# The second copy of the convolution weights: made by VectorE inside SBUF, or by DMA transfers

## The chip, the core and the metric

The kernel runs on one core of a Trainium2 chip. The metric is device time in microseconds (us) for one execution; less is better. A core has five engines that run side by side and wait for each other by semaphores: TensorE (PE in the profile, with its weight loads as PEld), VectorE (DVE), ScalarE (ACT), GpSimd (POOL) and SyncE (SP), which here issues the DMA transfers. SBUF is the on-chip memory of 128 partitions; PE writes its results to PSUM, which here is used as eight banks.

## The reference

An image x of 1 x 224 x 224 pixels and 96 channels is convolved with a 7 x 7 kernel w of 96 x 96 channels, cyclically in both directions, by way of the Fourier transform, all in bf16 at the ends:

```python
wp = jnp.pad(w, ((0, H - K), (0, W - K), (0, 0), (0, 0)))
Xf = rfft2(x, axes=(1, 2)); Wf = rfft2(wp, axes=(0, 1))
Yf = jnp.einsum('bhwi,hwio->bhwo', Xf, Wf)
y = irfft2(Yf, s=(H, W), axes=(1, 2)).astype(jnp.bfloat16)
```

## The kernel before, in words

The kernel transforms along the rows of the image only (H, in blocks of 28 rows with 6 rows of overlap, 17 frequencies) and does the seven taps along W as a short convolution with fewer products. Per frequency there are up to three planes (real, imaginary and their combination), 50 slots in all, and per slot ten combined taps. The image goes through in seven tiles of 32 columns. In each tile 17 rounds, one for each frequency, multiply transformed pixels (J, xf) with transformed weights (WF); the sums (u, v, yf) go out to memory, come back in another order (tt), and are transformed back with a matrix G.

Every engine call goes through `call` at lines 87 to 92, which keeps the program order on each engine. So the profile gives line 88 for everything, and the groups are told apart by tiles: **wu** fillers, **wq** weights, **WF** transformed weights, **Fm** the transform matrix, **xf** transformed pixels, **J** their sums, **ct** small constants, **pb** a PSUM bank.

What the change touches is the head, before round 0:

- **Loads (178 to 197).** SyncE issues, in this order: the columns left of the image (xh), the first tile's pixels of the upper half (load_x(0, 0)), the weights, and the first tile's pixels of the lower half (load_x(0, 1)). The first tile's pixels lie in the late part of WF, which is needed only later. One queue takes them in turn.
- **The weights.** w has 49 taps of 96 x 96 channels. Tap r goes to row 2r of the tile wq: the last tap in two small transfers (185), the others in three pieces of the columns (188). The odd rows 2r + 1 hold the same weights moved by 48 output channels (C2): four transfers from wq to wq (189 to 192), each of which has to wait for its piece of w. With both copies one matmul handles two output channels at once: `prep_jobs` (349) takes a strided column o of wq as the stationary operand, for o in 0 to 47, and the matrix Em as the moving one, 98 rows contracted; Em (57 and 295) has zeros such that the even rows give the lower 48 output channels and the odd rows the upper 48. Each job makes four output pairs in one bank. The zeros behind the weights (zw, 228) let the stationary operand read 128 columns.
- **Constants.** POOL and DVE compute Fm, Em and G from iota, floors and sines. thp (245) is the tap's row, pm, twp, hf, mk, mk2 (265 to 275) the mask by tap and by parity of the row. `build_g` (299) makes G on POOL over many one-element operations, which end in a sine on ACT and a multiply on POOL (`fin`, 342), called at line 779. Small constants lie in the pool stmp, which is given back at line 780 for yf and the sums.
- **The order at the head (761 to 779).** Fillers on a zero tile, 8 and 9 (207), then the transform of the left columns (a_bank), the first tile's upper half (f_jobs, ten banks), then 20 fillers in three banks (769), then the first group of the weight transform (`prep_jobs(0)`, 12 banks of 4 matmuls), the first part of the lower half, and J of the first frequencies. The other weight groups are spread over the rounds by `add` and `pace`.
- **Who empties a bank (119).** `evac` gives a bank to DVE or ACT by two running accounts, load["v"] and load["a"], so what is booked on one engine pushes later banks to the other. The accounts are set anew at line 783, before the rounds.

Of the kernel before, what the change touches and what calls it, by code (L numbers as in the profile page):

```python
# [9 lines left out]
F32 = mybir.dt.float32  # L10
ALU = mybir.AluOpType
ACTF = mybir.ActivationFunctionType

KT = 7
B = 28
# [7 lines left out]
Q = 2 * LC  # L23
# [6 lines left out]
NTAP = 10  # L30
# [25 lines left out]
def kernel(  # L56
# [7 lines left out]
    _, H, W, C = x.shape  # L64
# [4 lines left out]
    R = HB + PAD  # L69
    PW = KT * KT  # L70
    FR = 2 * NS
    PW2 = 2 * PW
    C2 = C // 2
    assert NJ == 8
    SYNC = mybir.DependencyInfo(mybir.DependencyClass.Sync, mybir.DependencyReason.DATA)
# [57 lines left out]
    def dma(out_ap, in_ap):  # L133
        return DE.dma_start(out=out_ap, in_=in_ap)
# [40 lines left out]
    def load_x(t, jg):  # L175
        return load_rows(xbuf(t, jg), jg, t * 2 * TW, 2 * TW)

    wsrc = w.rearrange("kh kw i o -> (kh kw) (i o)")
    for jg in range(2):
# [2 lines left out]
    cuts = tuple((c * WC // 3, (c + 1) * WC // 3) for c in range(3))  # L182
    lr = PW - 1
    wp = WC // 16
    wdma = [dma(wqx[2 * lr:2 * lr + 1, 0:WC].rearrange("p (a h b) -> p a h b", a=8, h=2)[:, :, h],
                bass.AP(wsrc.tensor, wsrc.offset + lr * WC + h * wp, [[WC, 1], [2 * wp, 8], [1, wp]])) for h in range(2)]
    for c0, c1 in cuts:
        wdma.append(dma(wqx[0:2 * lr:2, c0:c1], wsrc[0:lr, c0:c1]))
    wdma.append(dma(wqx[2 * lr + 1:PW2, 0:WC - C2].rearrange("p (a b) -> p a b", a=16),
                    wqx[2 * lr:2 * lr + 1, C2:WC].rearrange("p (a b) -> p a b", a=16)))  # L190
    for c0, c1 in cuts:
        wdma.append(dma(wqx[1:2 * lr:2, max(c0 - C2, 0):c1 - C2], wqx[0:2 * lr:2, max(c0, C2):c1]))

    def beside_w(r):
        for d in wdma:
            tc.declare_no_dep(r.ins, d.ins, reason="columns behind the weights")
    load_x(0, 1)

    wu = cpool.tile([128, 128], BF16, name="wu")
# [9 lines left out]

    ntmp = [0]  # L210

    def ftile(shape):
        ntmp[0] += 1
        return stmp.tile(shape, F32, name=f"ct{ntmp[0]}")

    def iota(ap, pattern, base=0, cm=0):
        GE.iota(ap, pattern=pattern, base=base, channel_multiplier=cm, allow_small_or_imprecise_dtypes=True)
# [4 lines left out]
        VE.tensor_single_scalar(out=out_ap, in_=out_ap, scalar=MAGIC, op=ALU.subtract)  # L222

    pi_t = ftile([128, 1])
    VE.memset(pi_t[:], math.pi)
    dmy = ftile([128, 1])
    SE.activation(out=dmy[:], in_=pi_t[:], func=ACTF.Sin, bias=0.0, scale=0.0)
# [4 lines left out]
    twc = ftile([PW2, KT]); mf = ftile([R, JG, NS * 2])  # L232
    iota(nrj[:], [[-B, JG]], base=-1, cm=1)
    iota(pw_i[:], [[0, 1]], cm=1)
    iota(aa[:], [[2, NS], [0, 2]])
    iota(phf[:], [[0, NS], [LC // 2, 2]], base=LC // 2)
    iota(phe[:], [[0, NS], [-(LC // 2), 2]], base=LC // 2)
# [4 lines left out]
        eng.tensor_scalar(out=out_ap, in0=out_ap, scalar1=MAGIC, scalar2=MAGIC, op0=ALU.add, op1=ALU.subtract)  # L242

    VE.tensor_scalar(out=nrj[:], in0=nrj[:], scalar1=0.0, scalar2=float(LC - 1), op0=ALU.max, op1=ALU.min)
    floor_div(VE, thp[:], pw_i[:], 2 * KT)
    VE.memset(aa[:, 0, 1:2], float(LC))
    VE.memset(aa[:, NS - 1, :], 0.0)
    VE.memset(phf[:, 0:NS:NS - 1, 1:2], LC / 2.0)
# [4 lines left out]
    floor_div(VE, fl[:], qq[:], Q)  # L253
    VE.scalar_tensor_tensor(out=qq[:], in0=fl[:], scalar=-float(Q), in1=qq[:], op0=ALU.mult, op1=ALU.add)
    SE.activation(out=qq[:], in_=qq[:], func=ACTF.Sin, bias=pi_t[:R, :], scale=-2.0 * math.pi / Q)

    GE.memset(mf[:], 1.0)
    GE.affine_select(out=mf[:], in_=mf[:], pattern=[[-B, JG], [0, NS * 2]], compare_op=ALU.is_ge, fill=0.0, base=-1, channel_multiplier=1)
# [3 lines left out]
        o = mf[:, :, 2 * NS - 2 + r:2 * NS - 1 + r]  # L262
        GE.affine_select(out=o, in_=o, pattern=[[-B, JG], [0, 1]], compare_op=ALU.not_equal, fill=v, base=-n, channel_multiplier=1)
    iota(twc[:], [[1, KT]])
    pm = ftile([PW2, 1]); twp = ftile([PW2, 1]); hf = ftile([PW2, 1]); mk = ftile([PW2, NTAP]); mk2 = ftile([PW2, 2, NTAP])
    th14 = ftile([PW2, 1])
    GE.tensor_single_scalar(out=th14[:], in_=thp[0:PW2], scalar=-2.0 * KT, op=ALU.mult)
    GE.tensor_tensor(out=pm[:], in0=th14[:], in1=pw_i[0:PW2], op=ALU.add)
    floor_div(GE, twp[:], pm[:], 2)
    GE.tensor_single_scalar(out=th14[:], in_=twp[:], scalar=-2.0, op=ALU.mult)  # L270
    GE.tensor_tensor(out=hf[:], in0=th14[:], in1=pm[:], op=ALU.add)
    GE.tensor_scalar(out=mk[:, 0:KT], in0=twc[:], scalar1=twp[:, 0:1], scalar2=None, op0=ALU.is_equal)
    GE.tensor_tensor(out=mk[:, KT:NTAP], in0=mk[:, 0:6:2], in1=mk[:, 1:6:2], op=ALU.add)
    GE.tensor_scalar(out=mk2[:, 1], in0=mk[:], scalar1=hf[:, 0:1], scalar2=None, op0=ALU.mult)
    GE.tensor_tensor(out=mk2[:, 0], in0=mk[:], in1=mk2[:, 1], op=ALU.subtract)
    for xb in xh_bufs:
        GE.memset(xb[:, PAD * C:], 0.0)
    for xb in x0_bufs + xn_bufs:
# [12 lines left out]
    for r, k in ((0, KT - 1), (1, 0)):  # L291
        VE.tensor_single_scalar(out=pv[:, NS - 2, r:r + 1], in_=thp[0:PW2], scalar=float(k), op=ALU.is_equal)
    VE.tensor_tensor(out=pv[:, :, 2], in0=pv[:, :, 0], in1=pv[:, :, 1], op=ALU.subtract)
    ke = -(-512 // (NB * NTAP))
    for k0, k1 in ((0, ke), (ke, NSLOT)):
        beside_w(VE.tensor_tensor(out=Em[:, :, k0:k1], in0=pe3[:, k0:k1].unsqueeze(1).unsqueeze(3).to_broadcast([PW2, 2, k1 - k0, NTAP]),
# [2 lines left out]
    def build_g(nj):  # L299
        PG = nj * FR  # L300

        def floor_g(out_ap, in_ap, d):
            GE.tensor_scalar(out=out_ap, in0=in_ap, scalar1=1.0 / d, scalar2=-(d - 1) / (2.0 * d), op0=ALU.mult, op1=ALU.add)
            GE.tensor_single_scalar(out=out_ap, in_=out_ap, scalar=MAGIC, op=ALU.add)
            GE.tensor_single_scalar(out=out_ap, in_=out_ap, scalar=MAGIC, op=ALU.subtract)

        def mod_g(out_ap, in_ap, fl_ap, d):
            floor_g(fl_ap, in_ap, d)
            GE.tensor_single_scalar(out=out_ap, in_=fl_ap, scalar=-float(d), op=ALU.mult)
            GE.tensor_tensor(out=out_ap, in0=out_ap, in1=in_ap, op=ALU.add)  # L310
        p = ftile([PG, 1]); sp = ftile([PG, 1]); rm = ftile([PG, 1]); jp = ftile([PG, 1]); rr = ftile([PG, 1]); z = ftile([PG, 1])
        iota(p[:], [[0, 1]], cm=1)
        mod_g(rm[:], p[:], jp[:], FR)
        mod_g(rr[:], rm[:], sp[:], 2)
        GE.tensor_single_scalar(out=z[:], in_=sp[:], scalar=0.0, op=ALU.is_equal)
        zr = ftile([PG, 1]); ag = ftile([PG, 1]); pg = ftile([PG, 1]); amp = ftile([PG, 1]); pgt = ftile([PG, 1])
        GE.tensor_tensor(out=zr[:], in0=z[:], in1=rr[:], op=ALU.mult)
        GE.tensor_scalar(out=ag[:], in0=zr[:], scalar1=LC / 2.0, scalar2=sp[:, 0:1], op0=ALU.mult, op1=ALU.add)
        en = ftile([PG, 1]); ne = ftile([PG, 1]); tg = ftile([PG, 1])
        GE.tensor_single_scalar(out=en[:], in_=sp[:], scalar=NS - 1.0, op=ALU.is_equal)  # L320
        GE.tensor_scalar(out=ne[:], in0=en[:], scalar1=-1.0, scalar2=1.0, op0=ALU.mult, op1=ALU.add)
        GE.tensor_scalar(out=ag[:], in0=ag[:], scalar1=2.0, scalar2=ne[:, 0:1], op0=ALU.mult, op1=ALU.mult)
        GE.tensor_tensor(out=pgt[:], in0=rr[:], in1=zr[:], op=ALU.subtract)
        GE.tensor_tensor(out=pgt[:], in0=pgt[:], in1=ne[:], op=ALU.mult)
        GE.tensor_scalar(out=pg[:], in0=pgt[:], scalar1=LC / 2.0, scalar2=LC / 2.0, op0=ALU.mult, op1=ALU.add)
        GE.tensor_scalar(out=amp[:], in0=z[:], scalar1=-1.0 / LC, scalar2=2.0 / LC, op0=ALU.mult, op1=ALU.add)
        GE.tensor_tensor(out=amp[:], in0=amp[:], in1=ne[:], op=ALU.mult)
        GE.tensor_tensor(out=amp[:], in0=amp[:], in1=en[:], op=ALU.add)
        GE.tensor_scalar(out=tg[:], in0=rr[:], scalar1=B - 1.0, scalar2=PAD - 1.0, op0=ALU.mult, op1=ALU.add)
        GE.tensor_tensor(out=tg[:], in0=tg[:], in1=en[:], op=ALU.mult)  # L330
        GE.tensor_single_scalar(out=jp[:], in_=jp[:], scalar=2.0 * B, op=ALU.mult)
        GE.tensor_tensor(out=tg[:], in0=tg[:], in1=jp[:], op=ALU.add)
        nm = ftile([PG, nj, B]); jc = ftile([PG, nj, B]); msk = ftile([PG, nj, B]); fl = ftile([PG, nj, B]); th = ftile([PG, nj, B])
        iota(nm[:], [[0, nj], [1, B]], base=PAD - 1)
        iota(jc[:], [[2 * B, nj], [0, B]])
        GE.tensor_scalar(out=msk[:], in0=nm[:], scalar1=en[:, 0:1], scalar2=None, op0=ALU.mult)
        GE.tensor_tensor(out=msk[:], in0=msk[:], in1=jc[:], op=ALU.add)
        GE.tensor_scalar(out=msk[:], in0=msk[:], scalar1=tg[:, 0:1], scalar2=amp[:, 0:1], op0=ALU.is_equal, op1=ALU.mult)
        GE.tensor_scalar(out=nm[:], in0=nm[:], scalar1=ag[:, 0:1], scalar2=pg[:, 0:1], op0=ALU.mult, op1=ALU.add)
        mod_g(th[:], nm[:], fl[:], Q)  # L340

        def fin():
            SE.activation(out=th[:], in_=th[:], func=ACTF.Sin, bias=pi_t[0:PG, :], scale=-2.0 * math.pi / Q)
            GE.tensor_tensor(out=G.rearrange("p (j m) -> p j m", j=nj), in0=th[:], in1=msk[:], op=ALU.mult)
        return fin

# [415 lines left out]
    for jg in range(2):  # L762
        for f in a_bank(0, xf0, xh_bufs[jg], 0, 3, jg, 0):
            f()
    fj = [f_jobs(0, p) for p in range(3)]
    for p in range(3):
        for f in fj[p][0]:
            f()
    for n in (9, 9, 2):
        warm(n)  # L770
    for f in prep_jobs(0):
        f()
# [3 lines left out]
            tc.add_manual_dep(d.ins, last[0].ins.name, SYNC, reason="second tile's pixels later")  # L776
    for f in jit(0, 0):
        f()
    g_fin()
    stmp_cm.__exit__(None, None, None)  # L780
    yf_pool = ctx.enter_context(tc.tile_pool(name="yf", bufs=YBUF))
    tv_pool = ctx.enter_context(tc.tile_pool(name="tv", bufs=2))
# [34 lines left out]
    bursts[(NS + LAG - 3, 1)] = (2, 0)  # L817
    nburst = len(bursts)
    for r in range(NS + LAG):
        if r == 0:  # L820
            add(0, 4, fj[1][1] + fj[2][1])
        for p in range(3):
# [152 lines left out]
```

## Time and profile before

| what | us |
|---|---|
| median of 3 runs | 262.58 (261.45 to 262.92) |
| the profiled execution | 261.39 |
| its span, first to last instruction | 259.7 |
| PE busy | 250.1 (96% of the span) |
| DVE busy | 213.8 (82%) |
| ACT busy | 197.9 (76%) |
| POOL busy | 107.8 (42%) |
| granted PE clock, mean | 0.996 |

The profile is one execution, with times from the start of its span. A timeline line gives start, duration from the first to the last of a run of like instructions, engine, operation, output tile <- input tiles, shapes, count and, in brackets, the idle time before it and what ended it. A busy PE is not PE at its peak, since matmuls overlap. Where prose speaks of the trace's landings, it means the time at which the last of a transfer's 16 completion signals came.

### The profile page before, as it was taken

What the parts mean: (1) busy time and instruction counts of PE and PEld (TensorE: products, weight loads), DVE (VectorE), ACT (ScalarE), POOL (GpSimd) and SP (SyncE); (2) the same over time, 40 slices, a digit from 0 to 9 for tenths busy, and PEclk for the clock granted to TensorE, in tenths of its full rate; (3) what the DMA queues carried; (4) which work ended last, traced back from release to release, by engine and by line L of the source; (5) the groups of instructions that cost most, each with busy time, mean ns of one, the idle gap of its engine ahead of it and who ended that gap; (6) DMA issues with size and microseconds to landing.
All of it is one profiled execution on the core that took longest, in us unless ns stands there. A gap on an engine that the chain in (4) does not pass through costs nothing.

```text
span 259.7 us, 12201 instructions
## 1 busy us (share of the span) xinstructions
PE 250.1 (96%) x5156; PEld 234.3 (90%) x5156; DVE 213.8 (82%) x455; ACT 197.9 (76%) x499; POOL 107.8 (42%) x172
## 2 busy tenths in 40 slices
PE   8999998999999999999999999999999999999981
PEld 3679998999999999999999998999999999999961
DVE  5649999798978979977988788777978889889982
ACT  5548997668875667998988879989798886666662
POOL 7784123336446543334133322543133332555621
PEclk9999999999999999999999999999999999999998
DMA  6947010731111299888979549697969853595145
GB/s 166 254 126 208 24 49 3 209 113 48 48 48 61 96 254 194 247 237 254 284 213 231 161 122 301 197 264 159 321 232 208 225 172 135 142 172 165 53 117 177
DMA packets 41416, 43.44 MB, mean 167 GB/s; under 512 B 30836, under 2 KB 33104, under 8 KB 41362
## 3 DMA queue, kind: packets, MB, share of 16 engines
q1 hardware_dynamic: 41044, 41.98, 58.7%
q8 instruction: 40, 0.66, 1.1%
q0 software_dynamic: 192, 0.52, 0.7%
q10 hardware_dynamic: 126, 0.17, 0.2%
q14 instruction: 14, 0.11, 0.1%
HBM read 22.09 MB, written 19.66 MB: 161 GB/s over the span
## 4 chain that ended last, share of the span: by engine, by line
PE 82%; DVE 6%; issue 4%; ACT 3%; POOL 3%; DVEq 0%; POOLq 0%; ACTq 0%
PE pb L88 82%; POOL ct L88 2%; DVE J L88 2%; ACT WF L88 1%; DVE xf L88 1%; DVE u L88 1%; POOL yf L88 1%; DVE v L88 1%; DVE WF L88 1%; ACT xf L88 1%; DVE wq L88 1%; DVE yf L88 0%; ACT tt L88 0%; ACT tt__1860 L88 0%; ACT tt__1159 L88 0%
## 5 line engine op out<-in xcount | busy, mean ns | idle before, releaser
L88 PE MATMUL pb<-WF,J 96*128 96x96 bf16 x2782 | 160.4, 206 | 0.1
L88 PEld LDWEIGHTS <-J 96*128 96x128 bf16 x2782 | 136.5, 98 | 7.0 <-issue 0.2
L88 POOL TENSOR_TENSOR yf<-v,u 128x384 bf16<-128x384 f32 x70 | 69.8, 1011 | 124.1 <-issue 67.8
L88 ACT CAST xf<-pb 96x408 bf16<-96x408 f32 (+2 forms) x147 | 68.8, 487 | 8.7 <-PE pb L88 6.9
L88 PE MATMUL pb<-WF,xf 96*128 96x96 bf16 x991 | 61.4, 206 | 0.8 <-ACT xf L88 0.5
L88 DVE TENSOR_TENSOR J<-xf 96x1824 bf16<-96x1824 bf16 (+1 forms) x82 | 56.8, 732 | 0.1
L88 PEld LDWEIGHTS <-xf 96*128 96x128 bf16 x991 | 48.9, 98 | 1.4 <-ACT xf L88 0.6
L88 PE MATMUL pb<-Fm,xn 118*128 118x136 bf16 (+3 forms) x640 | 45.5, 199 | 0.8 <-DVE u L88 0.8
L88 ACT CAST WF<-pb 96x480 bf16<-96x480 f32 (+1 forms) x57 | 28.4, 579 | 4.7 <-PE pb L88 4.6
L88 PE MATMUL pb<-tt,Gm 102*84 102x384 bf16 (+1 forms) x132 | 32.0, 325 | 0.0
L88 PEld LDWEIGHTS <-xn 118*128 118x128 bf16 x640 | 30.5, 97 | 1.1 <-issue 1.0
L88 ACT CAST yo<-pb 84x384 bf16<-84x384 f32 (+1 forms) x65 | 27.8, 484 | 2.8 <-PE pb L88 2.8
L88 ACT CAST J<-pb 84x384 bf16<-84x384 f32 (+1 forms) x65 | 28.0, 484 | 2.5 <-PE pb L88 2.5
L88 DVE TENSOR_TENSOR J<-J 96x912 bf16<-96x912 bf16 (+2 forms) x41 | 22.8, 556 | 0.0
L88 PE MATMUL pb<-wq 98*128 98x120 bf16 (+1 forms) x288 | 21.3, 226 | 0.2 <-DMA wq<-wq 0.2
L88 PEld LDWEIGHTS <-wq 98*128 98x128 bf16 x288 | 19.4, 148 | 0.7 <-issue 0.7
L88 POOL TENSOR_TENSOR xn<-v,u 128x384 bf16<-128x384 f32 x12 | 10.9, 925 | 9.2 <-DVE J L88 6.2
L88 DVE CAST WF<-pb 96x480 bf16<-96x480 f32 (+1 forms) x15 | 8.8, 614 | 4.2 <-PE pb L88 4.0
L88 PE MATMUL pb<-wu 128*128 128x512 bf16 x39 | 10.8, 438 | 1.1 <-DVE ct L88 1.1
L88 DVE TENSOR_TENSOR yf<-v,u 128x384 bf16<-128x384 f32 x20 | 11.2, 558 | 0.7
L88 PEld LDWEIGHTS <-Gm 102*84 102x84 bf16 (+1 forms) x132 | 11.4, 118 | 0.2
L88 ACT COPY xf<-xf 96x816 bf16<-96x816 bf16 (+3 forms) x18 | 10.3, 630 | 0.0
(406 smaller groups left out, 253.5 us busy)
## 6 DMA issues: line engine op xcount, KB each, us to landing
scr<-yf SPq DMA_DIRECT2D x30, 288.0 KB
xn<-in_x_dram SPq DMA_DIRECT2D x12, 672.0 KB
tt<-scr SPq DMA_DIRECT2D x24, 336.0 KB
out_dram<-yo SPq DMA_DIRECT2D x12, 252.0 KB
out_dram<-J SPq DMA_DIRECT2D x12, 252.0 KB
tt<-scr SPq DMA_DIRECT2D x6, 288.0 KB
WF<-in_x_dram SPq DMA_DIRECT2D x2, 672.0 KB
scr<-yf SPq DMA_DIRECT2D x6, 192.0 KB
```

The lines of the kernel that those rows point to most:

```text
L88: r = fn(*a, **k)
```

## The change

The rows of wq are laid out anew: the weights themselves go to rows 64 to 112, the copy moved by 48 channels to rows 0 to 48, and rows 49 to 63 are a gap that has to be zero (cleared from row 32 on, before the copy is written). 113 rows are contracted instead of 98. The four transfers from wq to wq are gone. In their place `shift` makes three copies on DVE, one for each piece of the columns, after the fourth, seventh and tenth pixel bank; each books 600 on DVE's account. The gap is cleared by one copy on ACT and two memsets on DVE. The mask follows: POOL loses the operations on parity and gains a memset and two copies; DVE gains two operations for the tap index. 20 fillers become 4. G's last two operations move to the start of round 2, and the tiles they read (msk, th, and pi in pi_g) to pools that live longer.

```diff
-    PW2 = 2 * PW
+    UP = 64
+    PW2 = UP + PW
...
-    wdma = [dma(wqx[2 * lr:2 * lr + 1, 0:WC]...
+    wdma = [dma(wqx[UP + lr:UP + lr + 1, 0:WC]...
     for c0, c1 in cuts:
-        wdma.append(dma(wqx[0:2 * lr:2, c0:c1], wsrc[0:lr, c0:c1]))
-    wdma.append(dma(wqx[2 * lr + 1:PW2, 0:WC - C2].rearrange("p (a b) -> p a b", a=16),
-                    wqx[2 * lr:2 * lr + 1, C2:WC].rearrange("p (a b) -> p a b", a=16)))
-    for c0, c1 in cuts:
-        wdma.append(dma(wqx[1:2 * lr:2, max(c0 - C2, 0):c1 - C2], wqx[0:2 * lr:2, max(c0, C2):c1]))
+        wdma.append(dma(wqx[UP:UP + lr, c0:c1], wsrc[0:lr, c0:c1]))
...
+    def halves(p0, p1, c, o0):
+        return wqx[p0:p1, cuts[c][0]:cuts[c][1]].rearrange("p (i o) -> p i o", o=C)[:, :, o0:o0 + C2]
+
+    def shift(c):
+        load["v"] += 600
+        r = VE.tensor_copy(out=halves(0, PW, c, 0), in_=halves(UP, PW2, c, C2))
+        for k, d in enumerate(wdma[2:]):
+            if k != c:
+                tc.declare_no_dep(r.ins, d.ins, reason="other columns")
+
+    def gap(eng, c):
+        z = halves(32, UP, c, 0)
+        beside_w(SE.copy(out=z, in_=wu[32:UP, 0:1].unsqueeze(2).to_broadcast(list(z.shape))) if eng is SE else eng.memset(z, 0.0))
...
-    floor_div(VE, thp[:], pw_i[:], 2 * KT)
+    VE.tensor_scalar(out=p64[:], in0=pw_i[:], scalar1=float(UP), scalar2=-float(UP), op0=ALU.is_ge, op1=ALU.mult)
+    VE.tensor_tensor(out=ptap[:], in0=p64[:], in1=pw_i[:], op=ALU.add)
+    floor_div(VE, thp[:], ptap[:], KT)
...
     SE.activation(out=qq[:], in_=qq[:], func=ACTF.Sin, bias=pi_t[:R, :], scale=-2.0 * math.pi / Q)
+    gap(SE, 0)
...
-    GE.tensor_single_scalar(out=th14[:], in_=thp[0:PW2], scalar=-2.0 * KT, op=ALU.mult)
-    GE.tensor_tensor(out=pm[:], in0=th14[:], in1=pw_i[0:PW2], op=ALU.add)
-    floor_div(GE, twp[:], pm[:], 2)
-    GE.tensor_single_scalar(out=th14[:], in_=twp[:], scalar=-2.0, op=ALU.mult)
-    GE.tensor_tensor(out=hf[:], in0=th14[:], in1=pm[:], op=ALU.add)
-    GE.tensor_scalar(out=mk[:, 0:KT], in0=twc[:], scalar1=twp[:, 0:1], scalar2=None, op0=ALU.is_equal)
+    GE.tensor_scalar(out=th14[:], in0=thp[0:PW2], scalar1=KT - 1.0, scalar2=-float(KT), op0=ALU.min, op1=ALU.mult)
+    GE.tensor_tensor(out=pm[:], in0=th14[:], in1=ptap[0:PW2], op=ALU.add)
+    GE.memset(mk2[:], 0.0)
+    GE.tensor_scalar(out=mk[:, 0:KT], in0=twc[:], scalar1=pm[:, 0:1], scalar2=None, op0=ALU.is_equal)
     GE.tensor_tensor(out=mk[:, KT:NTAP], in0=mk[:, 0:6:2], in1=mk[:, 1:6:2], op=ALU.add)
-    GE.tensor_scalar(out=mk2[:, 1], in0=mk[:], scalar1=hf[:, 0:1], scalar2=None, op0=ALU.mult)
-    GE.tensor_tensor(out=mk2[:, 0], in0=mk[:], in1=mk2[:, 1], op=ALU.subtract)
+    GE.tensor_copy(out=mk2[0:UP, 1], in_=mk[0:UP])
+    GE.tensor_copy(out=mk2[UP:PW2, 0], in_=mk[UP:PW2])
...
+    for c in (1, 2):
+        gap(VE, c)
...
+    nf = 0
     for p in range(3):
         for f in fj[p][0]:
             f()
-    for n in (9, 9, 2):
+            nf += 1
+            if nf in (4, 7, 10):
+                shift((4, 7, 10).index(nf))
+    for n in (4,):
         warm(n)
...
-    g_fin()
...
     for r in range(NS + LAG):
+        if r == 2:
+            g_fin()
```

## The prediction

> **What bounds the kernel now.** I read the page's busy shares first: PE is busy for 96% of the span, so time can only be saved where PE stands or does work that computes nothing. PE's timeline of the first 45 us shows where that is (start, duration, instruction, count, and in brackets the idle time before and what ended it).
>
> ```profile
> 10.99 4.48 PE L88 MATMUL pb<-wu 128*128 128x512 bf16 x20
> 15.68 3.16 PE L88 MATMUL pb<-wq 98*128 98x128 bf16 x48 [0.21 <-DMA wq<-wq]
> 18.68 1.10 PE L88 MATMUL pb<-Fm,WF 118*128 118x64 bf16 x32
> 20.23 0.51 PE L88 MATMUL pb<-WF,xf 96*128 96x96 bf16 x8 [0.46 <-ACT xf L88]
> ...
> 43.51 0.95 PE L88 MATMUL pb<-Fm,xn 118*128 118x32 bf16 x32 [0.76 <-DVE u L88]
> ```
>
> The reader is to see that 20 fillers stand between 10.99 and 15.47, that the first wq matmul is released by the wq<-wq transfers, and that between 20.23 and 45 PE has one gap, at 42.7. SyncE's timeline gives the four wq<-wq issues (8.25 to 11.55), and the trace's landings the rest: the three pieces of w land at 8.78, 9.93 and 11.03, the four copies at 11.31, 12.35, 14.47 and 15.44. So the weights are there at 11.03 and PE waits for their shifted copy until 15.44. The stage is bound by that chain.
>
> Next, DVE's timeline, since DVE takes over the copy.
>
> ```profile
> 7.57 1.40 DVE L88 TENSOR_TENSOR wq<-ct,ct 98x140 bf16<-98x140 f32 x2 [1.83 <-POOL ct L88]
> 8.88 3.25 DVE L88 CAST xf<-pb 96x408 bf16<-96x408 f32 x6
> 16.15 2.08 DVE L88 CAST WF<-pb 96x400 bf16<-96x400 f32 x4 [4.01 <-PE pb L88]
> ```
>
> DVE waits 1.83 us for POOL's mask before Em, and stands from 12.14 to 16.15. From 20.7 to 44.7 it never waits more than 0.25 us at once: there DVE, not PE, sets the pace, and PE's gap at 42.7 ends with "DVE u". What DVE loses in that stage is lost to the end.
>
> **Removed.** Four transfers (15.44 no longer ends the wait); 16 fillers of 0.216 us, 3.45 us of PE, which cost nothing before because PE waited for the transfers anyway. The second half's pixels are issued behind w instead of behind the copies: they landed at 17.51 and 17.84. Now 672 KB follow 11.03 at the 262 GB/s of the w pieces (288 KB in 1.1 us), so 13.7; they are needed 3.0 us after the first wq matmul, 16.7. Hidden, with 3 us to spare. On SyncE only the second tile's pixels stand behind them, which wait for ACT until 19.7 in any case. Contracting 113 rows for 98: weight loads of 118 rows take 97 ns and of 96 rows 98 ns, so rows cost nothing.
>
> **DVE up to the copies.** Two dependent one-element operations more on the tap index, at the 0.33 us between such rows (1.19 to 1.52), make the chain about 0.45 us later, so what ended at 5.74 ends at 6.19. PE first needs Fm at 6.64; Fm ended at 5.33, so that is covered. POOL's mask loses three operations, about 1.1 us, and is ready near 6.4. The two gap memsets are 768 words each; the memset of 64 words took 0.112 us and of one 0.059, so 0.84 ns a word, 0.75 us each with the start: Em at 7.7 where it was 7.57. (Nothing below that: POOL's mask at 6.4 bounds the gain at 1.1; a memset at twice the price would cost 1.4 more.) The casts follow at their old distances (8.88, 9.37, 9.86, 10.46, 11.06): the fourth is done at 11.2. All of w but the last third is there, so copies 1 and 2 don't wait; a cast (0.60) lies between 2 and 3, and the third piece (11.03) is long there. These are added waits all the same: behind a copy that waited, the last pixel cast and the WF evacuations would stand, and PE behind these; the margins are 2.4 us for the first piece and 1.9 for the third. ACT's gap copy of 1536 elements, at the 0.92 ns of its 2072 element row, takes 1.4 us in an idle stretch of 2.56 us (to 7.02).
>
> **One copy** (49 partitions, 1536 bf16 each, SBUF to SBUF, one source) has no row. Lower end: the one-source f32 operation of 170 elements took 0.25 us, that of one element 0.154, so 680 bytes in 0.096 us; 3072 bytes then take 0.43 + 0.154 = 0.59. Middle: two-source bf16 rows, 1824 elements in 1.05 us from start to start, give 0.88. Upper end: the f32 row of 860 elements in 0.97 gives 1.7. I take 0.6, by the row of the same kind (one source, SBUF to SBUF, no PSUM): 0.5 from start to start, as casts start 0.08 before the end of the last, and 0.1 for meeting POOL's one-element operations. Sum: 11.2 + 3 x 0.6 + 0.6 + 0.1 to PE = 13.7, against 15.68: **-1.95**.
>
> **From there to round 0.** PE's 48 wq matmuls and 32 Fm matmuls are as before (62 and 32 ns apart). Of the twelve evacuations ACT now has seven, DVE five, since the copies are booked to DVE's account: ACT ends one 0.46 us later but starts 0.26 earlier, so the first convolution is 0.2 later by this: 18.5 instead of 20.23, -1.75. DVE's last xf cast comes 2.05 earlier, and its J operations start at 18.7 instead of 20.75. ACT's sine for G (0.37, and 0.76 of waiting for POOL) leaves this place for round 2, and POOL's Gm multiply (0.70) with it; they are needed by no round of the first half.
>
> **POOL beside DVE.** G's chain on POOL ran until 20.90. It starts 1.1 earlier and loses about as much to the copies, so it still runs at 18.7 when DVE's J operations start. These rows show what such company costs:
>
> ```profile
> 37.69 2.14 DVE L88 TENSOR_TENSOR WF<-WF 96x960 bf16<-96x960 bf16 x3
> ...
> 40.68 1.96 DVE L88 TENSOR_TENSOR J<-xf 96x1824 bf16<-96x1824 bf16 x2
> ```
>
> The first of the three WF operations ran beside POOL's yf (37.18 to 38.18) and took 1.01, the others 0.64 each; the J operation of 40.68 ran beside the yf of 40.37 and took 1.65, where 20.75 took 1.12 alone. DVE waits out the POOL operation. Three J operations against POOL operations of 0.26 to 0.44 us: up to 1.0 us, where Gm and the halo copies cost 0.46 before (0.470 for 0.307, 0.766 for 0.464): **+0.55**, between 0 and 1.0. The Trainium skill says more ("SBUF — State Buffer", section "Who interferes with whom"): the port pair that VectorE and GpSimd share is an exclusive lock, taken also by one-source copies in a two-port mode. That speaks against this change, whose copies run beside POOL's chain; the rows agree on two-source operations, and no row of before shows a copy. Without such a lock the sum would be the rival of free ports below, with it my own.
>
> **Sum**: -2.05 + 0.55 = -1.5 along DVE (along PE -1.75, of which PE's gap at 42.7 takes 0.25). Behind it the order is the same on every engine. The profiled execution took 261.39 (span 259.7 and 1.7 around it): 259.9. The median of the runs shown is 262.58, 1.2 above: **261.1**.
>
> **Rivals.** Of 262.58, 0.5% is 1.3 us, about what a measurement of this kernel can tell from no change.
> - Free ports: POOL's chain is done or passes between the J operations; nothing is lost there. -2.05: 260.5. For it: half a microsecond of POOL's work moves either way.
> - Copies at two elements a step: 0.88 and 0.1 of meeting POOL, 1.2 more in all, 262.3. For it: the two-source bf16 rows; against it: the f32 row.
> - POOL becomes the bound: the first yf sum on DVE waits for POOL's scratch. G's chain would end at 20.9 - 1.1 + 1.5 (copies) + 1.8 (J operations) = 23.1, DVE is there at 21.95: 1.15 lost, 262.2. Against it: this takes every operation blocked in full.
> - **Slower**: each copy goes at the pace of the 860 element row, 1.7 us. From 1.1 us a copy on the gain is gone; at 1.7 it is 3.3 - 1.5 = +1.8: 264.4. Its place is DVE between 11.2 and the first wq matmul, which would start at 17.0.
> - The clock falls: PE ends its four fillers at about 11.5 and stands 2.2 us. At the end of the trace the granted clock still reads 1.00 up to 257 us and 0.50 from 258, with PE's last matmul over at 254.4, so 3.1 us of rest were needed. Fillers at the start came 0.427 us apart and 0.216 after 4.9; 3.9 us at half speed would cost 1.9: +0.4, 263.0. The Trainium skill ("TensorE: Matmul & The Clock Gate", "What's actually happening") puts the fall after an idle window of about 3.4 us, on windows that run freely; by that rule 2.2 us of rest keeps the clock, and the trace agrees.
>
> **Chances.** Forecast 0.50; with its spread of 0.5 us about 1.5, I count 0.34 of it beyond 1.3 and 0.16 within. Free ports 0.12, two a step 0.12, POOL the bound 0.08, slow copies 0.13, clock 0.05. Faster by over 0.5%: 0.34 + 0.12 = 0.46. Within: 0.16 + 0.12 + 0.08 + 0.05 = 0.41. Slower: 0.13. The range runs from free ports less 0.6 (259.9), about the spread of the runs shown, to the fallen clock and a little more (263.2), and leaves out the slow copies and a few hundredths below.
>
> **What would show it.** Three wq<-wq copies on DVE between 11 and 13.7, 0.5 to 0.6 each; the first wq matmul near 13.7, released by DVE; the first convolution near 18.5; J operations of about 1.3, 0.6 and 0.7; PE's gap near 41 grown to 1.0; clock 1.00 throughout. Wrong if a copy takes over 1 us, if wq matmuls come over 80 ns apart, or if PE has a new gap behind 20 us.

## The result, and the profile after

The changed kernel takes 263.40 us (median of 22 runs, 260.96 to 265.89), the kernel before 261.75 (22 runs, 260.98 to 263.33); the ratio is 1.0041, with an interval of 1.0023 to 1.0059. Forecast were 261.1 and a range of 259.9 to 263.2 for a kernel at 262.58. So it was to gain 1.5 us and loses 0.6 to 1.5 by the ratio. Executions whose granted clock is low from start to end, or that lie over 1.5% above the fastest (265.89 here, 414.53 with 16 fillers, 412.23 and 282.86 of the kernel before with 4), are left out of the ratios. The profiled execution took 263.59, its span is 261.9 where it was 259.7.

PE's timeline of the changed kernel, with the same stages as the lines shown of before:

```profile
10.96 1.02 PE L89 MATMUL pb<-wu 128*128 128x512 bf16 x4
14.57 5.33 PE L89 MATMUL pb<-wq 113*128 113x128 bf16 x48 [2.59 <-DVE wq L89]
19.70 1.42 PE L89 MATMUL pb<-Fm,WF 118*128 118x64 bf16 x32
21.56 0.51 PE L89 MATMUL pb<-WF,xf 96*128 96x96 bf16 x8 [0.44 <-ACT xf L89]
...
45.19 0.95 PE L89 MATMUL pb<-Fm,xn 118*128 118x32 bf16 x32 [0.80 <-DVE u L89]
```

Two things went otherwise than forecast. The first wq matmul starts at 14.57, not 13.7; that is still 1.1 earlier than before. And the 48 matmuls take 5.33 us where they took 3.16. That is what loses: the first convolution is at 21.56, 1.3 later than before. DVE's timeline has the reason of the first:

```profile
7.59 1.39 DVE L89 TENSOR_TENSOR wq<-ct,ct 113x140 bf16<-113x140 f32 x2
8.90 2.26 DVE L89 CAST xf<-pb 96x408 bf16<-96x408 f32 x4
11.19 0.56 DVE L89 COPY wq<-wq 49x1536 bf16<-49x1536 bf16 x1
12.36 0.56 DVE L89 COPY wq<-wq 49x1536 bf16<-49x1536 bf16 x1 [0.61 <-DMA wq<-in_w_dram]
12.84 0.68 DVE L89 CAST xf<-pb 96x512 bf16<-96x512 f32 x1
13.96 0.56 DVE L89 COPY wq<-wq 49x1536 bf16<-49x1536 bf16 x1 [0.45 <-DMA wq<-in_w_dram]
```

The copies cost what was forecast, but the second and third wait for w. By the trace's landings the pieces of w are there at 10.35, 12.34 and 13.94; before, at 8.78, 9.93 and 11.03. The table of stretches has the reason of the second. Its columns are the stretch, its length, the busy time of PE, its weight loads, DVE, ACT and POOL (with counts), then the granted PE clock, the DMA share and GB/s. First the kernel before, then the changed one:

```profile
7.00:9.00 2.00, 1.44 (x40) 1.34 (x39) 1.40 (x3) 1.36 (x3) 1.82 (x12) 1.00 1.03 261
9.00:11.00 2.00, 1.96 (x73) 1.85 (x69) 2.00 (x4) 1.64 (x5) 1.41 (x8) 1.00 0.86 222
```

```profile
7.00:9.00 2.00, 2.00 (x42) 1.66 (x40) 1.93 (x4) 1.09 (x3) 1.67 (x5) 1.00 1.10 170
9.00:11.00 2.00, 2.00 (x77) 1.94 (x74) 2.00 (x4) 2.00 (x6) 1.42 (x8) 1.00 1.05 160
11.00:13.00 2.00, 0.98 (x9) 0.25 (x5) 1.35 (x4) 0.67 (x2) 1.68 (x5) 1.00 0.98 147
13.00:15.00 2.00, 0.42 (x4) 0.43 (x5) 1.06 (x2) 0.00 (x0) 1.50 (x7) 0.64 0.88 226
15.00:20.00 5.00, 5.00 (x52) 5.00 (x51) 2.77 (x5) 2.92 (x7) 4.31 (x13) 0.50 0.03 8
```

Two columns carry it. GB/s: while w moves, 147 to 170 instead of 222 to 261, with the DMA engines as busy as before. Clock: 0.50 from 15 to 20 us. The trace's clock record has the fall at 13.57 and the rise at 20.40; before, the clock stood at 1.00 from 4.93 to 257.5.

**The theory that the runs test.** Two causes, each to be tested by itself. *Rows*: transfers to 49 neighbouring rows go at little more than half the rate of the rows 0, 2, ... 96 of before, so w comes 1.6 to 2.9 us later. *Clock*: with 4 fillers PE rests so long that the clock falls; a late w makes the rest longer. The rivals: w is late for another reason (queue, other transfers), the matmuls are slow for another reason (113 rows, data written by VectorE), and what DVE gains is lost to POOL, as the forecast had it.

### The profile page after: what moved, and what is told of

It reads as the page before. It is cut to its first block, busy times and chain, and to the rows that moved or that the text cites. A ratio compares the mean times of both kernels' runs of the same rounds, so it can differ in the third digit from the quotient of the medians.

```text
span 261.9 us, 12170 instructions
## 1 busy us (share of the span) xinstructions
PE 250.1 (95%) x5140; PEld 235.5 (90%) x5140; DVE 216.5 (83%) x461; ACT 200.5 (77%) x502; POOL 106.4 (41%) x169
## 4 chain that ended last, share of the span: by engine, by line
PE 84%; DVE 5%; DMA 3%; issue 2%; ACT 2%; SPq 2%; POOL 0%; DVEq 0%
PE pb L89 84%; DMA wq<-in_w_dram 3%; SPq L89 2%; DVE WF L89 1%; DVE xf L89 1%; DVE J L89 1%; DVE u L89 1%; DVE v L89 1%; ACT xf L89 1%; ACT WF L89 1%; POOL yf L89 0%; ACT tt L89 0%; DVE wq L89 0%; ACT tt__1845 L89 0%; DVEq L89 0%
## 5 line engine op out<-in xcount | busy, mean ns | idle before, releaser
L89 POOL TENSOR_TENSOR yf<-v,u 128x384 bf16<-128x384 f32 x70 | 69.1, 1001 | 126.9 <-issue 69.9
L89 ACT CAST xf<-pb 96x408 bf16<-96x408 f32 (+3 forms) x148 | 69.2, 490 | 6.9 <-PE pb L89 3.3
L89 PE MATMUL pb<-wq 113*128 113x120 bf16 (+1 forms) x288 | 23.6, 241 | 2.6 <-DVE wq L89 2.6
L89 PEld LDWEIGHTS <-wq 113*128 113x128 bf16 x288 | 21.5, 152 | 3.1 <-DVE wq L89 3.1
L89 PEld LDWEIGHTS <-Gm 102*84 102x84 bf16 (+1 forms) x132 | 11.4, 118 | 0.7 <-DMA tt<-scr 0.5
L89 DVE TENSOR_TENSOR yf<-v,u 128x384 bf16<-128x384 f32 x20 | 11.2, 558 | 0.7
L89 DVE TENSOR_TENSOR WF<-WF 96x960 bf16<-96x960 bf16 x14 | 9.8, 746 | 0.1
```

The source lines that it names most:

```text
L89: r = fn(*a, **k)
```

## The experiments

The table sums up all traces: when the last piece of w landed, the first wq matmul started, how long the 48 took, the first convolution, and by how much DVE's instructions between 100 and 220 us come later (+) or earlier (-) than the same instructions of the kernel before. This shift is constant to 0.01 us over nearly all of that stretch, so it measures the head more sharply than the total does. It is that of one execution, though: with the same transfers of w (changed, after_b, fill16, fill10, gfin) the last piece landed between 13.10 and 14.55. Behind 225 us some traces show up to 1 us more; in one of them (fill10) PE waits 0.66 us there for one transfer (tt<-scr). That may make much of the scatter of the totals.

| run | fillers | w | first wq | 48 take | convolution | shift |
|---|---|---|---|---|---|---|
| before | 20 | 11.03, copies 15.44 | 15.68 | 3.16 | 20.23 | 0 |
| changed | 4 | 13.94 | 14.57 | 5.33 | 21.56 | +1.56 |
| after_b | 4 | 14.12 | 14.75 | 3.19 | 19.49 | -0.55 |
| fill16 | 16 | 13.70 | 14.34 | 3.11 | 19.00 | -1.02 |
| fill10 | 10 | 14.55 | 15.19 | 3.11 | 19.85 | -0.18 |
| gfin | 16 | 13.10 | 13.78 | 3.09 | 18.42 | -1.63 |
| before4b | 4 | 10.97, copies 16.21 | 16.55 | 5.03 | 22.96 | +2.79 |
| xfer | 20 | 13.12, copies 19.04 | 19.28 | 4.54 | 25.22 | +5.18 |
| low | 16 | 13.82 | 14.64 | 3.17 | 19.36 | -0.78 |
| split | 12 | 14.78 | 16.80 | 3.16 | 21.51 | +1.41 |
| split2 | 12 | 13.12 | 13.76 | 3.16 | 18.46 | -1.56 |

### The clock: the number of fillers alone

```diff
-    for n in (4,):
+    for n in (8, 8):
```

> The changed kernel with 16 fillers (two banks of 8) in place of 4, nothing else. PE then ends its fillers at 10.96 + 16 x 0.216 = 14.4, just before the copies are done (14.53). Theory clock: what the change loses is the half clock after PE's rest of 2.6 us. Then the granted clock stays 1.00 through the head in every run, the 48 wq matmuls take 3.1 us and not 5.3, the first convolution comes near 14.6 + 4.8 = 19.4 (before 20.23, after 21.56), and the time is 0.6 to 0.9 us under the kernel before, with runs as close together as those of before. Rival collisions: the loss lies in the stage that DVE paces behind round 0 (POOL's chain beside the J operations). Then the time stays at 0.4% over the kernel before, or worse, since the J operations now come while POOL still works on G.

Measured: 261.17 us (median of eleven) beside 262.03 of the kernel before, ratio 0.9966 (0.9951 to 0.9982). PE's lines in this kernel:

```profile
10.60 3.61 PE L89 MATMUL pb<-wu 128*128 128x512 bf16 x16
14.34 3.11 PE L89 MATMUL pb<-wq 113*128 113x128 bf16 x48
17.29 1.10 PE L89 MATMUL pb<-Fm,WF 118*128 118x64 bf16 x32
19.00 0.51 PE L89 MATMUL pb<-WF,xf 96*128 96x96 bf16 x8 [0.62 <-ACT xf L89]
```

Twelve matmuls that compute nothing turn a loss into a gain: 0.75% between the two ratios, some 2 us. The wq matmuls with 113 rows take 3.11 us, so neither the rows nor VectorE's writing made them slow.

```diff
-    for n in (4,):
+    for n in (10,):
```

> The changed kernel with 10 fillers in one bank: PE works to 13.1 and then rests 1.45 us instead of 2.6. Theory clock with free running windows of 3.41 us: the half clock comes in fewer runs than with 4 fillers, so the median lies between that of 16 fillers and that of 4, and single runs fall into two heaps about 2 us apart. Rival (rest of over 3.1 us needed, as I read the end of the trace of before): neither 1.45 nor 2.6 us of rest can halve the clock, and 4, 10 and 16 fillers give the same time within 0.3 us.

Measured: 260.92 us, ratio 0.9962 (0.9945 to 0.9980). PE rests 1.39 us ahead of the wq matmuls, and the clock stays at 1.00. The times of 10 and 16 fillers can't be told apart. So the two heaps that the theory expected here did not come, and the rival is out as well, since 4 fillers do differ.

The same cut, made in the kernel before:

```diff
-    for n in (9, 9, 2):
+    for n in (4,):
```

> The kernel before with 4 fillers in place of 20, nothing else: PE rests from 11.9 to 15.7, 3.8 us. Theory clock: the clock is halved in most or all runs, the 48 wq matmuls take 5 to 6 us, and the kernel is 1.5 to 3 us slower than before. Rival: the fillers are idle work, and the time is that of before within 0.3 us.

Measured: 264.54 us (median of four), ratio 1.0097 (1.0077 to 1.0117). For its lines the same kernel ran once more:

> The kernel before with 4 fillers instead of 20, one look. Theory: PE stands from 11.9 to 15.7 us, the granted clock falls to 0.5 for at least one window of 3.41 us, the wq matmuls come about 108 ns apart instead of 62, and the first convolution is 1.3 to 2 us later than 20.2: 264 to 265 us. Rival (what the forecast assumed of fillers): wq matmuls 62 ns apart at clock 1.0, 261.5 us.

Measured: 265.15 us (one run). PE's lines:

```profile
10.96 1.02 PE L88 MATMUL pb<-wu 128*128 128x512 bf16 x4
16.55 5.03 PE L88 MATMUL pb<-wq 98*128 98x128 bf16 x48 [4.56 <-DMA wq<-wq]
21.41 1.10 PE L88 MATMUL pb<-Fm,WF 118*128 118x64 bf16 x32
```

With nothing else changed, 16 fillers fewer cost 1%. The clock record falls at 14.23, 2.2 us behind the last filler, and rises at 21.06. (In this execution the last copy of w also landed 0.77 later, so 0.87 of the 2.73 us by which the first convolution is late lie ahead of the first wq matmul.) So the fillers, which hid behind the transfers and looked free, kept the clock. Last, the changed kernel itself once more:

> The changed kernel once more, one look. Theory: the clock is decided in windows of 3.41 us that start anywhere; with 2.6 us of rest the same program loses no, one or two windows of half clock, about 261.0, 262.5 or 264 us; the landings of w (10.4, 12.3, 13.9) don't depend on it. Rival: the wq matmuls are slow for another reason (113 rows, or reading what VectorE wrote): then they are 108 ns apart in each run.

Measured: 261.68 us. The rest was 2.35 us and the clock stayed at 1.00:

```profile
14.75 3.19 PE L89 MATMUL pb<-wq 113*128 113x128 bf16 x48 [2.35 <-DVE wq L89]
17.77 1.10 PE L89 MATMUL pb<-Fm,WF 118*128 118x64 bf16 x32
```

So the same program has both outcomes, and its 22 runs show them: 260.96, 261.01 and 261.47 with a mean clock of 0.998 or more, five of 263.59 to 264.48 with 0.981 or 0.982, and of the others, with 0.986 to 0.993, all but one (265.89) between 261.03 and 263.96.

### The rows: where w is written

The rows of the changed kernel, but the copy by four transfers as before, 20 fillers, and the lower pixels behind them:

```diff
+    xfer = [dma(wqx[lr:lr + 1, 0:WC - C2]..., wqx[UP + lr:UP + lr + 1, C2:WC]...)]
+    for c0, c1 in cuts:
+        xfer.append(dma(wqx[0:lr, max(c0 - C2, 0):c1 - C2], wqx[UP:UP + lr, max(c0, C2):c1]))
+    load_x(0, 1)
...
-                shift((4, 7, 10).index(nf))
-    for n in (4,):
+    for n in (9, 9, 2):
```

> The changed kernel's rows (weights in 64 to 112, the moved copy in 0 to 48) with the copy made by four transfers as before, lower pixels behind them, and 20 fillers. Theory rows: the pieces of w land late because rows 64 to 112 take them at half the pace: 10.4, 12.3 and 13.9 as in the changed kernel (8.8, 9.9 and 11.0 before), though nothing stands behind them in the queue. The copies then land near 18 and the kernel is over 2 us slower than before. Rival queue: the pieces are late because the lower pixels follow them at once; here they land at 8.8, 9.9 and 11.0.

Measured: 266.87 us, ratio 1.0196 (1.0172 to 1.0219). With the kernel before's order of transfers, w still lands late, at 10.23, 12.07 and 13.12, and at the low rate:

```profile
7.00:9.00 2.00, 1.64 (x40) 1.46 (x39) 1.93 (x4) 1.24 (x3) 1.67 (x5) 1.00 1.05 173
9.00:11.00 2.00, 2.00 (x76) 1.94 (x73) 2.00 (x4) 1.70 (x5) 1.42 (x8) 1.00 0.98 147
```

What differs from before at this point is the rows, and the zeroing of the gap, which is over at 7.6 us while the rate stays low. The copies between these rows are slow as well (19.04 instead of 15.44), PE rests 3.9 us, and the clock falls here too. Is it that the rows lie above 64, or that all lie on one side of it, or that they are neighbours? Neighbours as such are not slow: between 4 and 6 us of the same trace the upper half's pixels, which go to the neighbouring rows 6 to 117 on both sides of 64, move at 289 GB/s. The next kernel is turned upside down: w to rows 0 to 48, VectorE copies up.

```diff
-        wdma.append(dma(wqx[UP:UP + lr, c0:c1], wsrc[0:lr, c0:c1]))
+        wdma.append(dma(wqx[0:lr, c0:c1], wsrc[0:lr, c0:c1]))
...
-        r = VE.tensor_copy(out=halves(0, PW, c, 0), in_=halves(UP, PW2, c, C2))
+        r = VE.tensor_copy(out=halves(UP, PW2, c, 0), in_=halves(0, PW, c, C2))
...
-    GE.tensor_copy(out=mk2[0:UP, 1], in_=mk[0:UP])
-    GE.tensor_copy(out=mk2[UP:PW2, 0], in_=mk[UP:PW2])
+    GE.tensor_copy(out=mk2[0:UP, 0], in_=mk[0:UP])
+    GE.tensor_copy(out=mk2[UP:PW2, 1], in_=mk[UP:PW2])
```

> The changed kernel with 16 fillers, turned upside down: w goes to rows 0-48, VectorE copies up to rows 64-112 (the zeroing of the gap moves ahead of the transfers). Theory: 49 neighbouring rows reach only a part of the paths that rows spread over 0-96 reach, wherever they lie; the pieces then land 1.7 to 2.0 us apart as with rows 64-112, the first wq matmul is at 13.8 to 15. Rival: rows from 64 on are slow by themselves; then the pieces land 1.1 us apart as in the kernel before (near 9.4, 10.5, 11.6), and the first wq matmul comes right behind the fillers, at 14.2.

Measured: 261.04 us (one run); the pieces land at 10.42, 12.41 and 13.82, at 147 to 154 GB/s between 9 and 13 us:

```profile
9.00:11.00 2.00, 2.00 (x83) 2.00 (x80) 1.97 (x5) 1.91 (x5) 1.50 (x8) 1.00 1.03 147
11.00:13.00 2.00, 2.00 (x23) 1.05 (x20) 1.07 (x2) 1.02 (x3) 1.64 (x6) 1.00 1.01 154
```

Rows 0 to 48 are as slow as 64 to 112; what the fast rows of before had, and the rows of the pixels, was that they lay on both sides of 64. The Trainium skill ("SBUF — State Buffer", section "Door 1: The DMA port swizzle") says just that: bandwidth depends on how many of the 16 ports the partitions reach, and partitions 0 to 63 reach eight of them, 64 to 127 the other eight. The rates agree (150 for 261), and no run shows the ports themselves.

If so, writing both sides at once should help. First by a second queue: the middle piece goes by ACT's queue to rows 0 to 48 and is copied up, the others stay (with G's sine in round 5, see below, and 12 fillers).

```diff
+    def split():
+        mid.append(SE.dma_start(out=wqx[lr:PW, m0 - C2:m1 - C2]..., in_=wsrc[lr:PW, m0:m1]...))
+        mid.append(SE.dma_start(out=wqx[0:lr, m0 - C2:m1 - C2], in_=wsrc[0:lr, m0:m1]))
...
+        if c == 1:
+            low = wqx[0:PW, m0 - C2:m1 - C2].rearrange("p (i o) -> p i o", o=C)[:, :, 0:C2]
+            r = VE.tensor_copy(out=halves(UP, PW2, c, 0), in_=low)
```

> As the run with the later sine, with 12 fillers, and the middle third of w goes by ACT's queue to rows 0-48 (already shifted), from where VectorE copies its first half up to rows 64-112. Theory: transfers to rows 64-112 alone go at 150 GB/s because they reach only part of what rows over the whole height reach (262 GB/s in the kernel before); the two queues then fill rows 0-48 and 64-112 at once, the first two thirds land by 10.5, the last by 12.3 instead of 13.7, the first wq matmul is at 13.1, the first convolution near 17.8, the time about 1.2 us under the run with the later sine: ratio 0.990. Rival: 150 GB/s is what w's transfers get at this place whatever their rows (queue order, other transfers); then the pieces land at 12.3, 12.3 and 13.9 and the ratio stays at 0.995, or is worse by ACT's time for the issue (0.5 us).

Measured: 262.14 us, ratio 1.0028 (1.0003 to 1.0053): a miss. The piece on ACT's queue, issued 6.8 to 7.8, was not moved beside the first one: its first packet moved at 9.44, beside the third piece. The first landed at 10.31, the third at 11.64, the middle one at 14.78, and DVE's second copy waited 3.12 us for it:

```profile
14.87 0.57 DVE L89 COPY wq<-wq 49x1536 bf16<-49x1536 bf16 x1 [3.12 <-DMA wq<-in_w_dram]
```

The time thus tells nothing of the rows, but the trace points the same way as the rates above: from 10 to 11.6 us, with the third piece going to the upper rows and the middle one to the lower, the two queues moved 192 GB/s together, about half each (some of SP's share may be the lower pixels already). Then in SP's one queue, between the other two:

```diff
+    wdma.append(dma(wqx[UP:UP + lr, 0:m0], wsrc[0:lr, 0:m0]))
+    mid.append(dma(wqx[lr:PW, m0 - C2:m1 - C2]..., wsrc[lr:PW, m0:m1]...))
+    mid.append(dma(wqx[0:lr, m0 - C2:m1 - C2], wsrc[0:lr, m0:m1]))
+    wdma.append(dma(wqx[UP:UP + lr, m1:WC], wsrc[0:lr, m1:WC]))
```

> The changed kernel with 12 fillers; the middle third of w, in SP's queue between the other two, goes to rows 0-48 (already shifted) and is copied up from there; the other two go to rows 64-112. In the changed kernel the 16 parts of one piece land over 2.1 us, as long as a piece takes, so some parts of the middle piece should move to the lower rows while others still move to the upper ones. Theory of the rows: the last piece then lands between 11.6 (262 GB/s throughout) and 13.0, the first wq matmul is at 13.2 behind the fillers, the time 0.8 to 1.2 us under that of 16 fillers: ratio 0.992 to 0.994. Rival: all parts move together and only one half of the rows is written at a time: 13.7 as before, ratio 0.9966 or a little worse, as the zeroing ahead of VectorE's chain makes that 0.75 later.

Measured: 260.36 us, ratio 0.9944 (0.9926 to 0.9963), the lowest of all, though its interval overlaps those of 16 and 10 fillers. The pieces land at 9.78, 11.31 and 13.12, and the rate is between the two:

```profile
7.00:9.00 2.00, 1.04 (x30) 0.89 (x28) 1.93 (x4) 1.01 (x3) 1.65 (x5) 1.00 1.00 201
9.00:11.00 2.00, 2.00 (x80) 1.99 (x77) 1.97 (x5) 2.00 (x6) 1.50 (x8) 1.00 1.05 197
11.00:13.00 2.00, 2.00 (x12) 0.88 (x9) 1.77 (x3) 0.72 (x2) 1.61 (x6) 1.00 0.95 160
```

While upper and lower rows are both in flight (until 11.3) it is 197 to 201, with the last piece alone 160. The last landing is a little beyond what was expected (13.0 at the latest), and landings scatter from run to run (13.10 in gfin), so the time alone would not prove the rows; the rate by stretch does.

### The sine of G

With 16 fillers DVE's instructions at 27 us come 1.27 earlier than before, from 32.6 on only 0.88. Between them lies this on ACT, then this on DVE:

```profile
27.73 0.37 ACT L89 ACTIVATE ct<-ct,pi_g 102x84 f32<-102x84 f32 x1
28.00 0.39 ACT L89 ACTIVATE tt__796<-pb 128x288 f32<-128x288 f32 x1
```

```profile
31.46 0.68 DVE L89 CAST xf<-pb 96x512 bf16<-96x512 f32 x1
32.64 0.36 DVE L89 SCALAR_TENSOR_TENSOR u<-pb,tt__918 128x192 f32<-128x192 f32 x1 [0.50 <-ACT tt__918 L89]
```

ACT sets the pace there, and the moved sine stands in its row. The test moves it on, and with it POOL's multiply Gm, which is issued by the same call:

```diff
-        if r == 2:
+        if r == 5:
             g_fin()
```

> The changed kernel with 16 fillers, and G's sine on ACT (0.37 us) issued in round 5 instead of round 2. With 16 fillers every operation of DVE from 25.5 to 31.5 us came 1.27 us earlier than in the kernel before, and from 32.6 on only 0.88: between them ACT takes the sine, and DVE then waits 0.50 us for ACT's tt. Theory: the sine moved into a stretch where ACT sets the pace costs 0.4 us of the end; in round 5 ACT waits 1.5 us for PE, so there it costs nothing. Then PE's gap ends 1.27 us ahead of the kernel before (near 42.2 instead of 43.5; 23.2 us behind the first convolution, not 23.6), and the time is 0.3 to 0.4 us under that of 16 fillers: ratio 0.995. Rival (what the forecast counted): VectorE loses the 0.4 us to POOL's operations on shared ports; then 23.6 us stay and the ratio stays at 0.9966.

Measured: 260.96 us, ratio 0.9975 (0.9959 to 0.9991); expected was 0.995. In the trace the loss at this place goes down from 0.38 to 0.16, but DVE loses 0.18 at 39 us, in J operations (2.14 us for two, 1.96 before). Beside them POOL now does the multiply Gm, in 1.24 us where it took 0.36 in round 2. PE's gap ends 23.6 us behind the first convolution, as the rival said, and not 23.2. From 20 to 100 us the shift falls by 0.37 (-2.00 to -1.63), with the sine in round 2 by 0.41 (-1.43 to -1.02). Split2, with the sine in round 2, has its first convolution 0.04 later than gfin and its shift 0.07 later. So the sine costs where it was put, as the trace shows, but taking it away gains next to nothing: other waits, the one beside POOL's multiply among them, take its place.

## Why the prediction was wrong, point by point

- **One copy, 0.6:** 0.56. Right, and the rivals of 0.88 and 1.7 are out.
- **DVE up to the copies:** Em at 7.59 (7.7), the fourth cast done at 11.16 (11.2), the two memsets 1.50 together (0.75 each), ACT's gap copy 1.47 (1.4) in an idle stretch. Right, though the tap index made DVE's chain 0.1 later and not 0.45.
- **"All of w but the last third is there, so copies 1 and 2 don't wait" and "rows cost nothing": the first step that failed.** The landings of before (8.78, 9.93, 11.03) were carried over to other rows unchanged; rows were weighed for PE alone, where they do cost nothing. Measured: 1.6, 2.4 and 2.9 later, the first wq matmul at 14.57 to 14.75 for 13.7. From after_b to gfin it moves by 0.97 and the shift by 1.08, so this is worth about 1 us in these two executions of the changed kernel. It is worth 0.1 in gfin, where w happened to land at 13.10, and 1.5 in fill10, where it landed at 14.55.
- **"16 fillers ..., which cost nothing before" and "2.2 us of rest keeps the clock": the second.** Fillers cost nothing where they stood, but their removal did. The forecast took the 3.1 us at the end of the trace for the rest that is needed, and the clock fell 1.6 us behind the last filler. That 3.1 was one draw: at the ends of the other traces the fall comes between 1.8 (fill16) and 5.2 us (before4b) behind PE's last matmul. Nor does the trace of before quite agree with a fall behind an idle window, as the forecast had it: the last 3.41 us ahead of its fall still held 0.31 us of PE's work. Worth some 2 us at the median (ratios 1.0041 and 0.9966). The clock was a rival, with a chance of 0.05 and 263.0, and its mechanism is what happened; w's delay lengthened the rest that it spoke of from 2.2 to 2.6 us. That its 263.0 is near the 263.40 measured is in part luck: it had no late w in it, and started from 262.58 where the kernel before now takes 261.75.
- **From the first wq matmul on:** right where the clock stays. In gfin and split2 it starts at 13.78 and 13.76, as forecast; the first convolution follows at 18.42 and 18.46 (18.5), J at 18.77 and 18.81 (18.7), and the shift is -1.63 and -1.56 (-1.5). So the sum lacked the two terms above. In the profiled execution the first wq matmul is 0.87 later than 13.7, and from there to the first convolution it takes 6.99 us where after_b takes 4.74: -1.5 + 0.87 + 2.25 = +1.62, and its shift is +1.56.
- **+0.55 for J beside POOL:** the size about right, the mechanism wrong. In fill16 and gfin the three J operations take 1.39 and 0.46 beside G's chain, no more than in the kernel before (1.51 and 0.77); POOL's four operations beside them take 2.44 us instead of 1.81. Here POOL waits, not DVE. (In the changed kernel itself G's chain is over by then, and the first J operation takes 1.42 us beside POOL's copies xf<-xf, 1.12 before.) What is lost, 0.4, is lost on ACT and later, and the sine, which the forecast moved to round 2 at no cost, is part of it.
- **The lower pixels hidden:** right, by less. They landed at 16.13 in fill16, 1.2 us ahead of their first use, where 3 were forecast.

What stays open: how little work brings the clock down (in the last section, it falls behind 0 to 1.82 us of work in 3.41, and twice stays up behind 1.43 and 1.67); and how much of the 0.4 each wait between 20 and 45 us would give back.

## What to carry to other kernels

Where a change moves data to other partitions, forecast its transfers anew: the rate belongs to the rows written, and rows on one side of 64 had little more than half of it. Before matmuls that compute nothing are taken out, ask what the clock does without them: here a rest of 1.39 us did no harm in eleven executions, and one of 2.6 cost about 2 us in the median, so cover a rest ahead of a dense stretch, with a margin for late transfers. And compare the same instruction between two traces, behind the changed stage: a shift that is constant to 0.01 us tells what a total with 1 us of scatter can't, for the two executions compared.

## What the hardware showed that was not expected

- The clock fell without a rest as long as at the end of the trace. In the changed kernel it stayed at 1.00 for 6.83 us, at 0.50 for 6.83 and then at 1.00 for 238.9; all are multiples of 3.413 us. It fell 1.59 us behind the last filler, and PE had worked 1.8 of the 3.41 us ahead of the fall. With 4 fillers before (before4b) it fell 2.2 us behind, in xfer 3.9; it did not fall in after_b (2.35 us of rest) nor in the profile of split (2.04), of whose other executions five have a mean clock of 0.986 to 0.992. The Trainium skill ("TensorE: Matmul & The Clock Gate", section "What's actually happening") has windows of 3.4 us that run freely, and the records agree; its rule that an idle window brings the fall does not hold for the changed kernel, where no such window was idle.
- Besides its length, it matters where the rest lies in these windows. In each trace the record changes only whole steps of 3.413 us behind its first entry, so PE's work can be counted step by step. In the changed kernel's profile 1.59 us of the rest lie in one step (10.16 to 13.57, 1.82 us of work), and the clock falls at its end. In after_b a step ends at 13.27, in the middle of the rest; the steps on both sides of it keep 2.54 and 1.94 us of work, and the clock stays. In eleven traces (all but before4's) no step with 1.94 or more was followed by a fall; all 14 falls stand behind 0 to 1.82. Two steps with less, 1.43 in split and 1.67 at the end of before4b, kept the clock, so busy time alone does not give the limit.
- POOL's operations beside VectorE's copies and J operations stretch (two of one element 0.73 to 0.96 us at 11.4, 0.49 before), and VectorE's copies keep their 0.56 us.
- Of two queues, the one on ACT started late: its piece, issued from 6.79 to 7.76 us, moved its first packet at 9.44, and then shared the rate about equally with SP's third piece (from 10 to 11.6 us).
